# A fused two-layer kernel: the last attention segment without memory, token factors ahead of the output projection, another PSUM bank for the closing pass, closing rows kept in PSUM

## The chip, the cores and the metric

The kernel runs on one core of a Trainium2 chip. The metric is the device time of one execution in microseconds; smaller is better. Matrix products run on TensorE (PE in the profile, its weight loads PEld), element-wise work on VectorE (DVE), ScalarE (ACT) and GpSimd (POOL), and transfers are issued from the queues of SyncE (SP), GpSimd and others. TensorE writes its results to PSUM, eight banks of 512 float32 values for each of 128 partitions; ScalarE and VectorE read them from there.

## What is computed

Two layers, A (attention with a recurrent memory) and B (a gated MLP that mixes over the sequence), each run twice over x of 2048 rows by 512. A goes through 64 segments of 32 rows, and 8 rows of memory pass from each segment to the next, so the segments form a chain. The core of the reference:

```python
def _A_ref(x, mem0, Wq, Wk, Wv, Wo, seg_len):      # 32 heads of 128, M = 8, seg_len = 32
    mem = mem0
    for s in range(n_seg):                          # 64
        h = concatenate([mem, xs], axis=1)          # 8 + 32 rows
        q, k, v = (einsum('btd,dhe->bhte', h, W) for W in (Wq, Wk, Wv))
        p = softmax(where(mask, q @ k * scale, -1e9))
        o = einsum('bhte,hed->btd', p @ v, Wo)
        mem = o[:, :M, :]
        outs.append(o[:, M:, :])
def _B_ref(x, w_in, w_sp, b_sp, w_out):
    z = gelu(einsum('bsd,df->bsf', x, w_in))
    z1, z2 = z[..., :Fh], layernorm(z[..., Fh:])
    return einsum('bsf,fd->bsd', z1 * (einsum('ts,bsf->btf', w_sp, z2) + b_sp), w_out)
x = x + A(layernorm(x)); x = x + B(layernorm(x))    # twice
```

The memory rows that the last segment would pass on go nowhere: only rows 8 to 39 of its output are returned.

## The kernel before

`kernel` builds one program; the function behind it calls `a_block` and `b_block` twice in turn. This document calls the first `a_block` block 1 and the second block 2. On TensorE, VectorE and ScalarE the order of the instructions is the order of the Python calls; on GpSimd and SyncE it is the scheduler's in `a_block`, and in `b_block` SyncE's order is that of the calls too.

`a_block` runs `segment(s, ...)` for s from 0 to 63. In a segment the projections are spread over the array in four column groups of 32, each matmul 32 columns wide by up to 512. A segment goes through these steps:

- Projections psQ (two tiles side by side), psm, psK and psV (line 721, `mm_chunk`). ScalarE casts them to `rows` (line 929), VectorE turns them into QQ and KA (line 932).
- Scores psS (lines 955 and 959), exponentials S (line 964), masked into E (line 967).
- `sums_ahead` and `sums_memory` (lines 990 and 981) give the softmax denominators of the memory queries, `sums_tokens` (line 999) those of the tokens, in psT. `pv` (lines 1007 and 1010) gives the weighted values psO, in two halves of 16 heads each.
- `memory_out` (lines 1024 to 1026) makes the memory's eight rows for uT: ScalarE takes the logarithm and the exponential of its negative, VectorE multiplies.
- The output projection of uT, which holds 24 token rows of the segment before and the 8 memory rows of this one: `wo_pairs` into px (line 798) and `wo_rest` into a corner of psO (line 805).
- The token factors Rt (lines 1090 and 1093), then `fold` (lines 894 and 896), `build_hA` (the memory for the next segment, lines 903 and 904), `store_o` (line 909), and the tokens' products `tok_out` and `last_out` (lines 1029 and 1032) into the next uT and into oB. oB collects the last 8 rows of each segment.

Into this chain other work is woven: `fill()` advances a generator that issues matmuls (projections of old rows, or `y_part`), `spare0` to `spare3` hold statistics and row sums, `copies`, `turns` and `adds` are lists of postponed closures, and `tail` and `loads` issue transfers.

`y_part(G, q, last)` projects the rows collected in oB for a group of 16 segments, a quarter of the heads at a time, into pwB (line 817). Its closure `out` runs with `adds` at the end of the segment and sums the quarters in yB in SBUF (lines 834 and 840), from where `store_last` writes them to o_d. For the last group (`last=True`, segments 61 to 63) three of the row sets get their heads 0 to 23 in three steps, and in each step a fourth column group takes 8 of the heads 24 to 31 of one set. After the loop the statistics and norms of the rows NB-6 and NB-5 are issued (lines 1237 to 1241; `y_norm` is line 249 on VectorE and the store of line 250), and then the closing pass: all 32 heads of the last uT and of the last row set into pw (line 1247). ScalarE copies pw to o_end (line 1250) and VectorE adds two pairs of 32 rows, reading pw and o_end (line 1253). Buffers named `ln_xn`, which `y_norm` writes, are two.

PSUM pools are opened in this order in `a_block`: one pool with accA (pwB and the old rows' projections) and accB (psm, psV, px, pw), one bank each; one with att (psQ, psS, psT; two banks) and the first psO (two banks); one with the second psO (two banks). `b_block` opens a pool of two banks for pg, then one with two buffers of three banks for pz. Its first instructions on TensorE are the 16 projections pz (line 296), each followed by GELU on ScalarE (line 297) and statistics on VectorE (line 300); after the first four, VectorE sums, norms and stores the last rows of x, which come back transposed as `front` for the last projections.

HALVED holds one base-36 digit per segment, the first string for block 1, the second for block 2: that many groups of four 512-wide matmuls in psK and psV are issued as eight of 256. The result is the same.

Of the kernel before, what the change touches and what calls it, by code (L numbers as in the profile page):

```python
# [14 lines left out]
P = 128  # L15
DM = 512
KT = 4
H = 32
# [12 lines left out]
HALVED = (  # L31
    "0380032975297907480707080708080707081904080708070807070807080708",
    "0529482947394739490607082903080708070807070906080729040807070807",
)
# [628 lines left out]
def a_block(tc, c, rows, front, MV_in, RS_in, MV_out, RS_out, ahead, wo, S, first):  # L663
# [6 lines left out]
    with ExitStack() as ctx:  # L670
# [86 lines left out]
        def run(todo):  # L757
            while todo:
                todo.pop(0)()
# [47 lines left out]

        yB, stores = {}, []

        def store_last(G, lo, hi, eng):  # L810
            eng.dma_start(o_d[512 * G + 4 * lo:512 * G + 4 * hi, :].rearrange("(j r) d -> j r d", r=32)[:, 24:32, :], yB[G][lo:hi, :])

        def wo_last(parts, pwB):

            for k, units in enumerate(parts):
                for t, (src, h) in enumerate(units):
                    nc.tensor.matmul(pwB[32 * t:32 * t + 32, :], lhsT=src[:, h, :], rhs=wo.head(h).rearrange("p (kt g el) -> p g kt el", kt=4, g=4),  # L817
                                     start=(k == 0), stop=(k == 7), tile_position=(0, 32 * t))
                yield

        def y_part(G, q, last=False):

            groups = [oBs[G][:, :, 32 * g:32 * g + 32] for g in range(4)]
            if last:
                parts = [[(groups[g], 8 * q + k) for g in range(3)] + [(groups[q], 24 + k)] for k in range(8)]
            else:
                parts = [[(groups[g], 8 * q + k) for g in range(4)] for k in range(8)]
            pwB = accA.tile([P, DM], F32, name="pwB")
            for k, _ in enumerate(wo_last(parts, pwB)):
                if k in (0, 3):  # L830
                    yield

            def add(lo, n, src):
                nc.vector.tensor_tensor(out=yB[G][lo:lo + n, :], in0=pwB[src:src + n, :], in1=yB[G][lo:lo + n, :], op=ALU.add)

            def out():
                n = 96 if last else P
                if q == 0:
                    yB[G] = wk.tile([P, DM], F32, name="yB", bufs=1)
                    nc.vector.tensor_copy(yB[G][0:n, :], pwB[0:n, :])  # L840
                else:
                    add(0, n, 0)
                if last:
                    if q == 2:
                        store_last(G, 0, 64, nc.sync)
                    add(32 * q, 32, 96)
                    if q == 2:
                        store_last(G, 64, 96, nc.sync)
                elif q == 3 and G < NB // 4 - 2:
                    stores.append(lambda: store_last(G, 0, P, nc.sync))  # L850
                elif q == 3:
                    store_last(G, 0, P, nc.sync)

            adds.append(out)
            yield

# [55 lines left out]
        def segment(s, fill, spare0, spare1, spare2, spare3, tail, loads):  # L912
# [155 lines left out]
            psT = att.tile([P, 2, 512], F32, name="psT")  # L1068
            sums = (psO[1][:, 0, 384:512].rearrange("p (g n) -> p g n", g=2), psO[1][:, :, 320:384])
            if not (first and s == 0):  # L1070
                fill()
            sums_ahead(sums[0])
            if not (first and s == 0):
                fill()
            pv(0)
            memory_out(0, sums[0])
            spare1(E)
            pv(1)
            sums_memory(1, sums[1])
            sums_tokens(psT)  # L1080
            memory_out(1, sums[1])
            run(copies)
# [5 lines left out]
            beside = nc.scalar.copy(cross[0:64, :], px[64:128, 128:256])  # L1088
            Rt = segp.tile([P, 2, 512], F32, name="Rt", tag="Rt", bufs=1)
            nc.scalar.activation(out=Rt[:], in_=psT[:], func=ACT.Ln)  # L1090
            for r in range(2):
                rt = Rt[:, :, 256 * r:256 * r + 256]
                nc.scalar.activation(out=rt, in_=rt, func=ACT.Exp, scale=-1.0)  # L1093
            run(turns)
            spare2()
            t1 = wk.tile([P, P], F32, name="t1", bufs=1)
# [5 lines left out]
            spare3()  # L1102
            tok_out(0)
            last_out(0)
            fill()
            run(copies)
            tok_out(1)
            last_out(1)
            run(adds)
# [132 lines left out]
        ends = (uT[NSEG % 2], oBs[NB // 4 - 1][:, :, 96:128])  # L1242
        pw = accB.tile([P, 512], F32, name="pw")
        for i in range(H // 2):
            for k in range(4):
                h = 2 * i + k % 2
                nc.tensor.matmul(pw[32 * k:32 * k + 32, :], lhsT=ends[k // 2][:, h, :], rhs=wo.head(h).rearrange("p (kt g el) -> p g kt el", kt=4, g=4),  # L1247
                                 start=(i == 0), stop=(i == H // 2 - 1), tile_position=(0, 32 * k))
        o_sb = segp.tile([P, DM], F32, name="o_end", tag="Rt", bufs=1)
# [45 lines left out]
```

## Time and profile before

| | |
|---|---|
| runs | 1621.28, 1623.1, 1629.42 us; median 1623.1 |
| the profiled execution | 1623.31 us, its span 1621.6 |
| TensorE busy | 1570.2 us, 97% of the span |
| weight loads / VectorE / ScalarE / GpSimd busy | 1003.5 / 1212.6 / 1062.5 / 294.4 us |
| granted TensorE clock, mean | 0.997 |
| closing pass pw, first start of each block | 691.22 and 1481.52 us |
| first pz behind it | 694.98 and 1485.34 us |

Times inside the span are counted from its start. In a row of the chain of waits stand start, length and the engine with the tile and the line. In a row of a timeline stand start, length from the first to the last of the merged instructions, engine, line, operation, output and inputs, and in brackets the idle time ahead of it with what ended it. In a row of windows stand the stretch, its length, then busy time (and count) of TensorE, its weight loads, VectorE, ScalarE and GpSimd, then the granted clock (1.00 is full), the share of the DMA engines and GB/s. A row of a DMA queue has packets, MB and the share of 16 engines' time.

### The profile page before, as it was taken

What the parts mean: (1) busy time and instruction counts of PE and PEld (TensorE: products, weight loads), DVE (VectorE), ACT (ScalarE), POOL (GpSimd) and SP (SyncE); (2) the same over time, 40 slices, a digit from 0 to 9 for tenths busy, and PEclk for the clock granted to TensorE, in tenths of its full rate; (3) what the DMA queues carried; (4) which work ended last, traced back from release to release, by engine and by line L of the source; (5) the groups of instructions that cost most, each with busy time, mean ns of one, the idle gap of its engine ahead of it and who ended that gap; (6) DMA issues with size and microseconds to landing.
All of it is one profiled execution on the core that took longest, in us unless ns stands there. A gap on an engine that the chain in (4) does not pass through costs nothing.

```text
span 1621.6 us, 94617 instructions
## 1 busy us (share of the span) xinstructions
PE 1570.2 (97%) x42719; PEld 1003.5 (62%) x42742; DVE 1212.6 (75%) x3181; ACT 1062.5 (66%) x2278; POOL 294.4 (18%) x604
## 2 busy tenths in 40 slices
PE   3899999999999999999999999999999999999999
PEld 1466666666666666656656666666666666665565
DVE  3677777778887888884467777777888788878722
ACT  2577777777777777662047777777777777776400
POOL 5111111112211221320011111111121112224000
PEclk9899999999999999999999999999999999999999
DMA  9322222123322334276972222221233223425697
GB/s 339 114 50 44 43 43 43 43 43 76 82 58 45 76 92 81 88 174 148 206 194 48 49 45 48 47 47 47 66 92 81 47 65 96 100 56 171 141 201 160
DMA packets 264764, 149.53 MB, mean 92 GB/s; under 512 B 198680, under 2 KB 240784, under 8 KB 264360
## 3 DMA queue, kind: packets, MB, share of 16 engines
q1 hardware_dynamic: 251128, 99.66, 28.4%
q0 software_dynamic: 13232, 43.82, 8.6%
q8 instruction: 335, 5.49, 1.4%
q14 instruction: 69, 0.57, 0.1%
HBM read 59.68 MB, written 37.19 MB: 60 GB/s over the span
## 4 chain that ended last, share of the span: by engine, by line
PE 55%; DVE 1%; ACT 1%; DMA 0%; issue 0%; DVEq 0%
PE pg L396 9%; PE psQ L721 7%; PE psK L721 7%; PE psb L721 5%; PE pz L296 4%; PE px L798 4%; PE psV L721 3%; PE psm L721 3%; PE psO L805 3%; PE py L439 2%; PE psO L1007 2%; PE pwB L817 1%; PE psT L999 1%; PE psS L955 1%; PE pw L1247 0%; PE psO L990 0%
## 5 line engine op out<-in xcount | busy, mean ns | idle before, releaser
L721 PEld LDWEIGHTS <-hT 128*32 128x32 bf16 x14372 | 377.4, 96 | 276.6 <-DVE hT L904 65.1
L932 DVE STREAM_TRANSPOSE QQ<-rows 128x512 bf16<-128x512 bf16 x256 | 179.5, 701 | 19.5 <-ACT rows L929 11.7
L932 DVE STREAM_TRANSPOSE KA<-rows 128x512 bf16<-128x512 bf16 x256 | 175.9, 687 | 13.5 <-ACT rows L929 12.8
L929 ACT CAST rows<-psQ 128x512 bf16<-128x512 f32 x256 | 142.3, 585 | 19.7 <-PE psQ L721 19.4
L396 PE MATMUL pg<-z,wspT 128*128 128x344 bf16 x1024 | 154.3, 309 | 0.0
L1029 DVE TENSOR_TENSOR uT<-psO,Rt 128x384 bf16<-128x384 f32 x256 | 141.4, 552 | 13.2 <-ACT Rt L1093 7.5
L1093 ACT ACTIVATE Rt<-Rt 128x512 f32<-128x512 f32 x256 | 147.3, 622 | 4.1
L1026 DVE TENSOR_TENSOR uT<-psO,Rm 128x128 bf16<-128x128 f32 x256 | 74.7, 292 | 98.1 <-ACT Rm L1025 51.6
L964 ACT ACTIVATE S<-psS 128x224 bf16<-128x224 f32 x256 | 91.6, 358 | 82.0 <-PE psS L959 82.0
L721 PE MATMUL psQ<-Wq_sb,hT 128*32 128x512 bf16 x2048 | 134.8, 381 | 7.3 <-ACT Rt L1090 5.1
L798 PEld LDWEIGHTS <-uT 128*32 128x32 bf16 x4608 | 111.6, 96 | 46.9 <-DVE uT L1026 32.9
L798 PE MATMUL px<-Wo,uT 128*32 128x256 bf16 x3840 | 135.3, 275 | 0.3 <-DVE uT L1026 0.3
L721 PE MATMUL psQ<-Wk_sb,hT 128*32 128x512 bf16 x2048 | 134.5, 381 | 0.0
L721 PE MATMUL psK<-Wk_sb,hT 128*32 128x256 bf16 (+1 forms) x2976 | 134.4, 313 | 0.0
L721 PE MATMUL psK<-Wv_sb,hT 128*32 128x512 bf16 (+1 forms) x2800 | 134.3, 322 | 0.0
L721 PE MATMUL psm<-Wq_sb,hT 128*32 128x512 bf16 x2048 | 134.0, 380 | 0.0
L721 PE MATMUL psV<-Wv_sb,hT 128*32 128x512 bf16 (+1 forms) x2452 | 133.4, 343 | 0.0
L1090 ACT ACTIVATE Rt<-psT 128x1024 f32<-128x1024 f32 x128 | 131.1, 1025 | 3.1
L396 PEld LDWEIGHTS <-wspT 128*128 128x128 bf16 x1024 | 100.2, 98 | 53.2
L805 PE MATMUL psO<-Wo_high,uT 128*32 128x128 bf16 x7168 | 124.7, 219 | 3.2 <-DMA Wo_high<-in_A_Wo_dram 2.3
L888 POOL COPY KX<-old 128x128 bf16<-128x128 bf16 x128 | 70.3, 553 | 314.9 <-PE psS L959 193.1
L888 POOL COPY KX<-front 128x128 bf16<-128x128 bf16 x126 | 67.7, 547 | 296.4 <-PE psS L959 223.0
(194 smaller groups left out, 2896.3 us busy)
## 6 DMA issues: line engine op xcount, KB each, us to landing
o_d<-o_sb SPq DMA_DIRECT2D x126, 64.0 KB
vb_d<-front SPq DMA_DIRECT2D x30, 256.0 KB
VX<-vb_d SPq DMA_DIRECT2D x120, 64.0 KB
ln_x<-xd SPq DMA_DIRECT2D x26, 256.0 KB
y_o<-o_d POOLq DMA_DIRECT2D x22, 256.0 KB, 3.3
xd<-y_o POOLq DMA_DIRECT2D x22, 256.0 KB, 3.5
Wq_sb<-in_A_Wq_dram POOLq DMA_DIRECT2D x8, 512.0 KB, 10.3
Wk_sb<-in_A_Wk_dram POOLq DMA_DIRECT2D x8, 512.0 KB, 11.5
```

The costliest lines, as they stand in the source:

```text
L396: nc.tensor.matmul(pg[t][:, k, 0:344], lhsT=wsp[t][:, st, :], rhs=z(st, 344 * k, 344 * k + 344), start=(st == 0), stop=(st == NT - 1))
L721: mms.append(nc.tensor.matmul(ps[32 * cg:32 * cg + 32, n * k:n * k + n], lhsT=lhs(kt, cg), rhs=r[:, m * k:m * k + m], start=(kt == 0), sto ...
L798: nc.tensor.matmul(px[at:at + 32, 0:256], lhsT=lhs[:, h, :], rhs=wo_rhs(h, slice(k + 2, None, -2) if h % 2 else slice(k, None, 2)), start= ...
L805: nc.tensor.matmul(pw[32 * cg:32 * cg + 32, :], lhsT=lhs[:, h, :], rhs=wo_rhs(h, cg), start=False, stop=(h == H - 1), tile_position=(0, 32 ...
L888: eng.tensor_copy(KX[:, :, r].rearrange("p g (k i) -> p i g k", i=4), bs["KTB"][:, r].rearrange("p (i g) k -> p i g k", i=4)[:, :, :, 8 * ...
L929: return r, mms, nc.scalar.copy(r[:], ps)
L932: nc.vector.transpose(out=QQ[:, j % 2, :, 0:32] if j < 2 else KA[:, j % 2], in_=r[:])
L964: return nc.scalar.activation(out=S[:, r], in_=psS[:, r, 0:224], func=ACT.Exp, scale=scale)
L1026: nc.vector.tensor_tensor(out=hview(uT_cur[:], r, 24, 32), in0=oview(r, 0, 8), in1=rm.rearrange("p g (n q) -> p g n q", q=8), op=ALU.mult)
L1029: nc.vector.tensor_tensor(out=hview(uT_nxt[:], r, 0, 24), in0=oview(r, 8, 32), in1=rview(r, 0, 24), op=ALU.mult)
L1090: nc.scalar.activation(out=Rt[:], in_=psT[:], func=ACT.Ln)
L1093: nc.scalar.activation(out=rt, in_=rt, func=ACT.Exp, scale=-1.0)
```

## The change

Four things are changed in `a_block`, and the strings.

- The last segment (`ends_here`) leaves out `sums_ahead`, `sums_memory` and both `memory_out`. The eight rows of uT that they filled keep older values; the output rows made from them are overwritten by `store_last`, as before.
- In the last segment the token factors are taken right behind psT, half 1 ahead of half 0, and the products `tok_out` and `last_out` of both halves go ahead of `fold` on VectorE.
- The closing pass writes to the first half of a tile of att instead of accB, and begins with heads 16 to 31.
- For the last group the three quarters keep one tile pwB. Its first three row sets accumulate in PSUM over all three segments; the fourth column group, started anew in each, is copied to yB by ScalarE. Only in segment 63 VectorE adds the 96 rows once, and one store of 96 rows follows.
- HALVED has new digits.

```diff
@@ -29,8 +29,8 @@
 WO_PAIR = 18
 LATE_STATS = 14
 HALVED = (
-    "0380032975297907480707080708080707081904080708070807070807080708",
-    "0529482947394739490607082903080708070807070906080729040807070807",
+    "5392919491949293909080707080708070807080708070708070807070807190",
+    "8084929392939050070807080708070708070807080707080708070807080708",
 )
 OLD_SIZES = (H * P, 8 * DH, H * 32, H * 32)
 ORDERED = {mybir.EngineType.PE, mybir.EngineType.DVE, mybir.EngineType.Activation}
@@ -805,17 +805,17 @@
                     nc.tensor.matmul(pw[32 * cg:32 * cg + 32, :], lhsT=lhs[:, h, :], rhs=wo_rhs(h, cg),
                                      start=False, stop=(h == H - 1), tile_position=(0, 32 * cg), skip_group_check=True)
 
-        yB, stores = {}, []
+        yB, stores, held = {}, [], {}
 
         def store_last(G, lo, hi, eng):
             eng.dma_start(o_d[512 * G + 4 * lo:512 * G + 4 * hi, :].rearrange("(j r) d -> j r d", r=32)[:, 24:32, :], yB[G][lo:hi, :])
 
-        def wo_last(parts, pwB):
+        def wo_last(parts, pwB, more=False):
 
             for k, units in enumerate(parts):
                 for t, (src, h) in enumerate(units):
                     nc.tensor.matmul(pwB[32 * t:32 * t + 32, :], lhsT=src[:, h, :], rhs=wo.head(h).rearrange("p (kt g el) -> p g kt el", kt=4, g=4),
-                                     start=(k == 0), stop=(k == 7), tile_position=(0, 32 * t))
+                                     start=(k == 0 and not (more and t < 3)), stop=(k == 7), tile_position=(0, 32 * t), skip_group_check=True)
                 yield
 
         def y_part(G, q, last=False):
@@ -825,8 +825,10 @@
                 parts = [[(groups[g], 8 * q + k) for g in range(3)] + [(groups[q], 24 + k)] for k in range(8)]
             else:
                 parts = [[(groups[g], 8 * q + k) for g in range(4)] for k in range(8)]
-            pwB = accA.tile([P, DM], F32, name="pwB")
-            for k, _ in enumerate(wo_last(parts, pwB)):
+            if not last or q == 0:
+                held["pwB"] = accA.tile([P, DM], F32, name="pwB")
+            pwB = held["pwB"]
+            for k, _ in enumerate(wo_last(parts, pwB, last and q > 0)):
                 if k in (0, 3):
                     yield
 
@@ -834,19 +836,19 @@
                 nc.vector.tensor_tensor(out=yB[G][lo:lo + n, :], in0=pwB[src:src + n, :], in1=yB[G][lo:lo + n, :], op=ALU.add)
 
             def out():
-                n = 96 if last else P
                 if q == 0:
                     yB[G] = wk.tile([P, DM], F32, name="yB", bufs=1)
-                    nc.vector.tensor_copy(yB[G][0:n, :], pwB[0:n, :])
+                if last:
+                    nc.scalar.copy(yB[G][32 * q:32 * q + 32, :], pwB[96:128, :])
+                    if q == 2:
+                        add(0, 96, 0)
+                        store_last(G, 0, 96, nc.sync)
+                    return
+                if q == 0:
+                    nc.vector.tensor_copy(yB[G][:], pwB[:])
                 else:
-                    add(0, n, 0)
-                if last:
-                    if q == 2:
-                        store_last(G, 0, 64, nc.sync)
-                    add(32 * q, 32, 96)
-                    if q == 2:
-                        store_last(G, 64, 96, nc.sync)
-                elif q == 3 and G < NB // 4 - 2:
+                    add(0, P, 0)
+                if q == 3 and G < NB // 4 - 2:
                     stores.append(lambda: store_last(G, 0, P, nc.sync))
                 elif q == 3:
                     store_last(G, 0, P, nc.sync)
@@ -1067,18 +1069,34 @@
             Rm = segp.tile([P, 2, 2, 64], F32, name="Rm", bufs=1)
             psT = att.tile([P, 2, 512], F32, name="psT")
             sums = (psO[1][:, 0, 384:512].rearrange("p (g n) -> p g n", g=2), psO[1][:, :, 320:384])
+            ends_here = s + 1 == NSEG
+            Rt = segp.tile([P, 2, 512], F32, name="Rt", tag="Rt", bufs=1)
+
+            def token_factors(rs):
+                nc.scalar.activation(out=Rt[:], in_=psT[:], func=ACT.Ln)
+                for r in rs:
+                    rt = Rt[:, :, 256 * r:256 * r + 256]
+                    nc.scalar.activation(out=rt, in_=rt, func=ACT.Exp, scale=-1.0)
+
             if not (first and s == 0):
                 fill()
-            sums_ahead(sums[0])
+            if not ends_here:
+                sums_ahead(sums[0])
             if not (first and s == 0):
                 fill()
             pv(0)
-            memory_out(0, sums[0])
+            if not ends_here:
+                memory_out(0, sums[0])
             spare1(E)
             pv(1)
-            sums_memory(1, sums[1])
+            if not ends_here:
+                sums_memory(1, sums[1])
             sums_tokens(psT)
-            memory_out(1, sums[1])
+            if ends_here:
+                spare2()
+                token_factors((1, 0))
+            else:
+                memory_out(1, sums[1])
             run(copies)
             px = accB.tile([P, 512], F32, name="px")
             wo_pairs(px, uT_cur)
@@ -1086,13 +1104,15 @@
             wo_rest(pw, uT_cur)
             cross = wk.tile([P, P], F32, name="cross", bufs=1)
             beside = nc.scalar.copy(cross[0:64, :], px[64:128, 128:256])
-            Rt = segp.tile([P, 2, 512], F32, name="Rt", tag="Rt", bufs=1)
-            nc.scalar.activation(out=Rt[:], in_=psT[:], func=ACT.Ln)
-            for r in range(2):
-                rt = Rt[:, :, 256 * r:256 * r + 256]
-                nc.scalar.activation(out=rt, in_=rt, func=ACT.Exp, scale=-1.0)
-            run(turns)
-            spare2()
+            if ends_here:
+                fill()
+                for r in (1, 0):
+                    tok_out(r)
+                    last_out(r)
+            else:
+                token_factors((0, 1))
+                run(turns)
+                spare2()
             t1 = wk.tile([P, P], F32, name="t1", bufs=1)
             fold(px, cross, t1, beside)
             if s + 1 < NSEG:
@@ -1100,12 +1120,14 @@
             if s > 0:
                 store_o(s, pw, t1)
             spare3()
-            tok_out(0)
-            last_out(0)
-            fill()
+            if not ends_here:
+                tok_out(0)
+                last_out(0)
+                fill()
             run(copies)
-            tok_out(1)
-            last_out(1)
+            if not ends_here:
+                tok_out(1)
+                last_out(1)
             run(adds)
             run(turns)
             tail()
@@ -1240,12 +1262,13 @@
         for y in (NB - 6, NB - 5):
             y_norm(y, nc.sync)
         ends = (uT[NSEG % 2], oBs[NB // 4 - 1][:, :, 96:128])
-        pw = accB.tile([P, 512], F32, name="pw")
-        for i in range(H // 2):
+        pw = att.tile([P, 2, 512], F32, name="pw")[:, 0, :]
+        for n in range(H // 2):
+            i = (n + H // 4) % (H // 2)
             for k in range(4):
                 h = 2 * i + k % 2
                 nc.tensor.matmul(pw[32 * k:32 * k + 32, :], lhsT=ends[k // 2][:, h, :], rhs=wo.head(h).rearrange("p (kt g el) -> p g kt el", kt=4, g=4),
-                                 start=(i == 0), stop=(i == H // 2 - 1), tile_position=(0, 32 * k))
+                                 start=(n == 0), stop=(n == H // 2 - 1), tile_position=(0, 32 * k))
         o_sb = segp.tile([P, DM], F32, name="o_end", tag="Rt", bufs=1)
         nc.scalar.copy(o_sb[:], pw[:])
         for k in range(2):
```

## The prediction

> **What bounds the kernel now.** I read the page, then the chain of waits around the end of both attention blocks, then the timelines of TensorE, VectorE and ScalarE there, and last the windows with the granted clock. The page says 97% busy TensorE, so only its idle stretches can be won or added. Most of the change lies in the last three segments and the closing pass of each attention block; the strings HALVED touch all segments. The chain at the end of the second block (start, us, what):
>
> ```profile
> 1460.05 0.60 DVE yB L840
> 1460.67 0.69 DVE yB L834
> ...
> 1461.93 0.67 DVE KA L932
> 1462.60 0.04 issue
> 1462.64 0.28 PE psS L955 x16
> ...
> 1478.28 0.37 issue
> ...
> 1481.04 0.43 DVE uT L1029
> 1481.47 0.04 issue
> 1481.52 3.83 PE pw L1247 x64
> 1485.34 2.43 PE pz L296 x12
> ```
>
> Two things are to be seen: VectorE's closing-row work (yB) delays the key transpose KA, for which the scores wait; and the closing pass pw waits for uT, behind px, ScalarE's Rt and VectorE's statistics. After pw, TensorE goes straight on to pz, the GELU projection of the next block. VectorE in the same stretch:
>
> ```profile
> 1483.68 0.55 DVE L249 TENSOR_SCALAR ln_xn<-rowsB,MV,RS 128x512 bf16<-128x512 f32 x1
> ...
> 1489.02 0.55 DVE L249 TENSOR_SCALAR ln_xn<-y_o,MV,RS 128x512 bf16<-128x512 f32 x1 [3.47 <-DMA xb_d<-ln_xn]
> 1489.60 1.40 DVE L1253 TENSOR_TENSOR o_end<-pw,o_end 32x512 f32<-32x512 f32 x2
> ```
>
> The two additions that read pw out of PSUM (L1253) end at 1491.00, 5.7 us after pz began at 1485.34: they stand behind three row normalisations (L249), the third of which waits until the first one's store has left its buffer. Before, nobody waits for them, since pw has a bank that pz doesn't use. In the first block: L1253 ends at 699.59, pz began at 694.98.
>
> **Part 1, rows kept in PSUM (gain).** Segments 61 and 62 each end with two VectorE instructions on yB (0.68 and 0.69), which fall into the transposes of the next segment. Starts of psQ put segment 61 at 10.02 us and segment 62 at 668.07 to 678.56, 10.49. From psQ to px: 7.39 in segment 61, 7.85 in 62 and 8.42 in 63. The change gives ScalarE one copy of 32x512 instead and VectorE one addition at the very end. Gain 0.46 + 1.03. The copy has no row: 0.26 is the copy of 64x128 (L1088), 0.57 that of 128x512 (L1250); since VectorE takes 0.68 for 32x512 and for 128x512 alike, length decides, and I take 0.55. It goes ahead of the next segment's first cast. In segment 62 ScalarE has 0.28 of idle time before the second and again before the third cast; VectorE, freed of 1.37, then starts its transposes no later than in segment 61, so the copy costs nothing. Without that cover it would cost 0.55.
>
> **Part 2, no memory in segment 63 (gain).** 16 L990 matmuls (0.12) and 4 L981 (0.06) go: 0.18. With part 1, px starts 1.6 earlier: about 685.4 and 1475.4. I count further from px.
>
> **Part 3, factors ahead of Wo.** psT is complete 0.2 after px starts; ScalarE, freed of four Rm steps (about 0.3 each), does Ln 1.02 and then the two Exp, 1.15 together: factors at 1.85 and 2.42. VectorE's two products for half 1 end at 2.5, for half 0 at 3.0. The closing pass now takes heads 16 to 31, half 1, first, so half 0 is needed only 1.9 later. TensorE needs px 1.10, L805 0.78, pwB 0.86 = 2.74 and can begin the closing pass there, where before it began 4.24 and 4.50 after px. pw ends at 2.74 + 3.83 = 6.57.
>
> **Part 4, the new bank (loss).** PSUM pools are opened in order: accA and accB take banks 0 and 1, att 2 and 3, the two psO 4 to 7. The next block opens a pool of two banks (0, 1) and then pz's two buffers of three banks, so the first pz lies in 2 to 4. pw moves from accB to att, bank 2. The first pz matmul overwrites pw and so must wait for every reader: ScalarE's copy and both L1253. Behind that wait on TensorE's queue stand all 16 projections, and for them wait GELU and the statistics on VectorE. When do the readers end? VectorE from 3.0 on: fold 0.8, o_sb 0.25, statistics 1.3, to 5.36; ScalarE then does Ln and Exp (0.56, as in block 2 from MV to RS) and only behind them, in program order, the closing copy 0.55, to 6.5; addition 0.68, to 7.2; first normalisation from 7.18. Before it stood at 6.40 and 6.66 after px, so of the 1.6 of parts 1 and 2 it keeps 0.8 and 1.1. The two stores of yB on SP's queue become one, an issue of 0.6 less ahead of the first normalisation's store; I count nothing for it. The third normalisation begins 3.69 (block 1) or 4.79 (block 2) after the first ended, by the rows 693.93 to 697.62 and 1484.23 to 1489.02; then 0.57 and 1.40. Readers end at 13.4 and 14.5 after px: 698.9 and 1490.0. pz is **later by 3.9 and 4.7**, and TensorE idles 6.9 and 8.0 us.
>
> **The clock after the idle time.** Windows of the start of the program (us, TensorE busy first, granted clock in the column 1.00 or 0.50):
>
> ```profile
> 48.50:51.90 3.40, 0.67 (x26) 0.50 (x26) 0.58 (x2) 1.64 (x3) 0.00 (x0) 1.00 0.93 314
> 51.90:55.35 3.45, 1.95 (x44) 1.18 (x47) 1.29 (x6) 0.80 (x2) 0.00 (x0) 0.50 0.05 17
> 55.35:58.75 3.40, 3.40 (x36) 1.27 (x32) 1.55 (x4) 1.13 (x2) 0.00 (x0) 0.50 0.00 0
> 721.50:724.90 3.40, 1.70 (x15) 1.15 (x13) 2.99 (x16) 3.22 (x4) 0.00 (x0) 1.00 0.79 140
> ```
>
> A stretch with 0.67 of 3.40 busy is followed by half the clock; one with 1.70 isn't. Idle times of 7 us contain a whole empty stretch, so pz restarts at 0.50. It stayed so for 3.4 us (45.1 to 48.5) and for 6.0 of work (52.79 to 58.75); half of that is lost, 1.7 to 3.0. I take **2.3 per block**, and as bounds 0 (no drop) and 3.0. The Trainium skill (TensorE: Matmul & The Clock Gate, Part 1: The HAM clock gate) states that the clock halves after one idle window of about 3.4 us and comes back after one busy window; by it the estimate is 1.7 per block, which would take 1.2 off the sum.
>
> **In block 1 a later wait gives some of it back.**
>
> ```profile
> 724.81 9.55 PE L296 MATMUL pz<-front 128*128 128x256 bf16 x80 [1.70 <-DMA front<-xb_d]
> ```
>
> TensorE waits here for rows that VectorE sums and normalises between the statistics of the first four z. TensorE's own delay would be 3.9 + 2.3 - 1.7 = 4.5. The row chain: the first projection (2.4 us, at half clock 4.7) ends at 703.6, the second at 706.05, its GELU (1.32) and statistics (1.1) at 708.6, and only then VectorE sums the first late row, which it began at 703.80 before; the four sums, the norms and the stores follow at their old distance: 4.8 to 5.0 later. The later ends last: block 1 **+5.0**. Block 2 has no such wait: 4.7 + 2.3 = **+7.0**.
>
> **Part 5, HALVED.** The page gives
>
> ```profile
> q8 instruction: 335, 5.49, 1.4%
> ```
>
> 5.49 MB over 335 packets is 16 KB, and over 85,461 weight loads and matmuls 64 bytes: 256 instructions per packet. Counted in order, the stalls "issue" inside segments (405.14, 425.17, 946.07, 1194.64, 1215.00, 1287.71, 1348.04, 1478.65 and others) stand at places 193 to 196 modulo 256, so at packet ends. Segments take 10.00 to 10.02 without one; over that, segments 16 to 61 lose 1.8 us in block 1 and 2.3 in block 2. A halved group adds 8 instructions at no TensorE time (psQ unhalved and psK often halved are both busy 134 us). Old and new digits both bring two segments to about 1280 instructions, five packets; what moves is where the packets end. Old packets last 4.4, 3.4, 4.8, 3.7 and 3.7 us, and the stalls sit on the 3.4 and the 3.7. New ones, by laying the new counts over the old rows: 4.6, 3.4 to 3.7, 4.4, 4.2 and 3.3. The shortest, from the VA loads to the next psQ, lasts 3.2 to 3.5 some 15 times before, with hardly a stall. I take **-1.5**, with the bounds -4.1 (no stall left) and +4.1 (twice as many). The Trainium skill (Runtime: NRT & Kernel Launch, Instruction fetch mechanics) calls the crossing of such a 16 KiB block mostly hidden; then this term is about 0. Here it costs up to 0.5 us where it isn't.
>
> **Sum.** The profiled execution took 1623.31 (span 1621.6); the median of the runs is 1623.1, the same within 0.02%. 5.0 + 7.0 - 1.5 = +10.5: **1633.8 us**.
>
> **Rivals.**
> 1. *The wait comes, the clock stays or the stores land early.* Without the clock term block 1 is bound by the row chain (+2.4) and block 2 by 4.7; with HALVED -1.5 that is +5.6: 1629. For it: idle times of 1.2 and 1.7 us left the clock alone. Against it: these are four times as long. 0.15.
> 2. *Other side: faster.* pz doesn't wait, because the first projection gets the other buffer or the readers come early. Place: the start of pz; price: all of part 4. Then block 2 gains 1.6 + 1.76 = 3.4; block 1 is held by the row chain, which moves 1.1; with HALVED -6.0: 1617.3. It decides once the readers end before pw's end plus 1 us; they end 7 later. For it speaks nothing in the rows but that pool order is argued from code. 0.10.
> 3. *HALVED goes wrong*: twice the stalls on top of the wait, 1633.8 + 5.6 = 1639.4. For it: the new shortest packet is 0.1 shorter than the old. 0.07.
>
> **Chances and range.** The forecast has 0.68. Its own range: pz start 1 us either way in each block, clock 1.7 to 3.0, HALVED by 2.5: 1629 to 1638.5. To hold 8 in 10 of all cases: 1627.5 to 1640. What can be told from no change is 0.5%, 8.1 us: slower means above 1631.2, faster below 1615. Slower: most of the forecast (0.58), rival 3 and a little of rival 1: 0.67. Faster: the tail of rival 2, 0.04. Same: 0.29.
>
> **What would show it.** TensorE's first pz row in each block with 6 to 8 us of idle time put down to DVE o_end; windows of 3.4 us behind it with the clock 0.50; psQ to px near 7.4 in segments 62 and 63 and 7.2 without memory; pw directly behind pwB; the wait for front about as long as before or longer; segments of 10.0. If pz follows pw at once, part 4 is wrong and the time is near 1617. If pz waits 7 us at full clock, rival 1 holds.

## The result, and the profile after

The changed kernel takes 1637.88 us (median of 6 runs, 1633.12 to 1640.96) where the kernel before takes 1622.19 (median of 6 runs, 1620.11 to 1629.42): the ratio is 1.0087, with a 95% interval of 1.0062 to 1.0113. So it is slower, by some 10 to 18 us. The profiled execution took 1640.96 us, its span 1639.2, 17.6 more than the span before.

The chain of waits of the kernel after, at the end of block 2 (start, us, what), shows the new path from the tokens' products to the next block:

```profile
1487.85 0.19 DVE uT L1031
...
1492.04 0.59 ACT yB L842
...
1493.26 0.53 DVE ln_xn L249
...
1495.13 3.67 DMA xb_d<-ln_xn
1498.80 1.85 issue
1500.65 2.72 PE pz L296 x6
```

Before, the chain ran uT, pw, pz on TensorE alone. Now pw isn't in it: between uT and pz stand the closing-row copy, a row norm and the transfer of that norm, then 1.85 us that the profile gives to nothing, in which VectorE ends the third norm and does the two additions. The same end in block 1, first VectorE's timeline, then TensorE's:

```profile
699.67 0.55 DVE L249 TENSOR_SCALAR ln_xn<-y_o,MV,RS 128x512 bf16<-128x512 f32 x1 [1.86 <-DMA xb_d<-ln_xn]
700.25 1.40 DVE L1276 TENSOR_TENSOR o_end<-pw,o_end 32x512 f32<-32x512 f32 x2
```

```profile
701.75 11.69 PE L296 MATMUL pz<-front 128*128 128x512 bf16 x48 [6.71 <-issue]
...
727.26 4.85 PE L296 MATMUL pz<-front,ln_x 128*128 128x256 bf16 x40
731.95 3.27 PE L296 MATMUL pz<-front 128*128 128x256 bf16 x27
```

The additions end at 701.65 and pz begins at 701.75: pz waits for them, though the row names only "issue": the trace has a wait instruction of TensorE at line 296 that ends at 701.70, 0.05 us behind the additions, and in block 2 it is the same (1500.59 behind 1500.55). The 48 matmuls behind the wait take 11.69 us instead of 9.47 for 47. The later wait for front, 1.70 us before, is gone, since TensorE itself is late. Windows there (length, busy TensorE, its weight loads, VectorE, ScalarE, GpSimd, then the granted clock) show why pz is slow:

```profile
695.40:698.80 3.40, 0.00 (x0) 0.00 (x0) 2.38 (x6) 1.28 (x4) 1.76 (x3) 1.00 0.53 157
698.80:702.20 3.40, 0.45 (x2) 0.20 (x3) 1.92 (x3) 1.08 (x1) 2.34 (x5) 0.60 0.48 144
702.20:705.60 3.40, 3.40 (x10) 1.26 (x9) 0.00 (x0) 0.00 (x0) 0.32 (x1) 0.50 0.67 252
```

Behind the counts stand the granted clock, the DMA share and GB/s. After one empty stretch the clock is half, and it stays so until about 4.4 us after pz has begun (0.50 up to 706.0, 1.00 from 706.5).

Cut at the first psQ of segments, the 17.6 us of span lie here. Each entry is the difference of such starts between the two traces.

| stretch | before | after | difference |
|---|---|---|---|
| up to the first psQ | 34.29 | 33.72 | -0.6 |
| block 1, segments 0 to 61 | 633.78 | 637.42 | +3.6 |
| block 1, segment 62 to the first psQ of block 2 | 167.98 | 172.02 | +4.0 |
| block 2, segments 0 to 61 | 621.99 | 625.55 | +3.6 |
| block 2, segment 62 to the end | 163.57 | 170.52 | +7.0 |

Two things had to be explained: the ends (+11.0) and the segments in between (+7.2), whose own instructions differ only in the digits HALVED (and, at the end of segment 61, in the copy of yB).

### The profile page after: what moved, and what is told of

Read it like the earlier page. It is cut to its first block, busy times and chain, and to the rows that moved or that the text cites. A ratio compares the mean times of both kernels' runs of the same rounds, so it can differ in the third digit from the quotient of the medians.

```text
span 1639.2 us, 94617 instructions
## 1 busy us (share of the span) xinstructions
PE 1575.4 (96%) x42742; PEld 1015.3 (62%) x42742; DVE 1208.3 (74%) x3167; ACT 1064.9 (65%) x2276; POOL 290.0 (18%) x604
## 4 chain that ended last, share of the span: by engine, by line
PE 93%; DMA 3%; DVE 2%; ACT 1%; issue 1%; POOL 0%; DVEq 0%; POOLq 0%
PE psQ L721 14%; PE psK L721 13%; PE psb L721 9%; PE pg L396 9%; PE px L798 8%; PE psm L721 7%; PE psV L721 6%; PE psO L805 6%; PE pz L296 5%; PE psO L1009 3%; PE pwB L817 3%; PE py L439 2%; PE psT L1001 2%; PE psS L957 2%; DMA Wk_sb<-in_A_Wk_dram 1%; DMA Wo_high<-in_A_Wo_dram 1%
## 5 line engine op out<-in xcount | busy, mean ns | idle before, releaser
L721 PEld LDWEIGHTS <-hT 128*32 128x32 bf16 x14404 | 386.4, 96 | 272.6 <-DVE hT L906 62.4
L721 PE MATMUL psK<-Wv_sb,hT 128*32 128x256 bf16 (+1 forms) x2812 | 135.0, 321 | 0.0
L805 PE MATMUL psO<-Wo_high,uT 128*32 128x128 bf16 x7168 | 123.5, 219 | 2.4 <-DMA Wo_high<-in_A_Wo_dram 2.4
## 6 DMA issues: line engine op xcount, KB each, us to landing
Wq_sb<-in_A_Wq_dram POOLq DMA_DIRECT2D x8, 512.0 KB, 10.7
```

What stands on the lines that cost most here:

```text
L721: mms.append(nc.tensor.matmul(ps[32 * cg:32 * cg + 32, n * k:n * k + n], lhsT=lhs(kt, cg), rhs=r[:, m * k:m * k + m], start=(kt == 0), sto ...
L805: nc.tensor.matmul(pw[32 * cg:32 * cg + 32, :], lhsT=lhs[:, h, :], rhs=wo_rhs(h, cg), start=False, stop=(h == H - 1), tile_position=(0, 32 ...
```

## The experiments

**e1, the old digits in the changed kernel; e2, the new digits in the kernel before.** At this point the theory (A) was that the digits cost by themselves what the table shows.

```diff
 HALVED = (
-    "5392919491949293909080707080708070807080708070708070807070807190",
-    "8084929392939050070807080708070708070807080707080708070807080708",
+    "0380032975297907480707080708080707081904080708070807070807080708",
+    "0529482947394739490607082903080708070807070906080729040807070807",
```

> The changed kernel with the strings HALVED of before; all else as changed. Theory A (the loss of 15.7 us is the two block ends, +4.1 and +7.3 in the profile, and the new digits, +3.5 and +3.2): block 1 from the first psQ to that of segment 63 takes about 644.2 us again instead of 647.8; block 2 is less sure, since 40 TensorE instructions less in block 1 shift where its packets end; the time falls by 3 to 7 us to about 1632. Theory B (the digits are neutral and the longer segments were the scatter of one execution): 1637 to 1639 and no difference in the segments beyond 1 us. The prediction's own term (new digits better by 1.5): 1639.4.

> The kernel before with the new strings HALVED and nothing else. Theory A: segments of block 1 cost about 3.5 us more, of block 2 about 3; time about 1622 + 3 to 7 = 1625 to 1629. Theory B: within 1 us of the kernel before. The prediction's own term: 1.5 us faster, 1620.7.

e1: 1639.74 us, ratio to before 1.010 (1.0085 to 1.0116): not faster than the change as made. e2: 1632.94, ratio 1.0061 (1.0042 to 1.0079), 10 us slower than before from digits alone. Neither is what theory A or its rival said. e1's time is near the 1639.4 that the prediction's own term gave for it: the old digits come out 1.9 us slower than the new ones in the changed kernel, though the two intervals overlap. By place, e1 has a good block 1 (segments 2 to 61 in 602.9 us against 605.0) and a bad block 2 (segments 0 to 61 in 626.5, against 625.5); e2 has a very bad block 2, 634.7, with the same digits that took 625.5 in the changed kernel. What differs between these two for block 2 is only what stands ahead of it: the changed kernel issues 20 matmuls less in segment 63, which is 40 TensorE instructions with their weight loads, so its block 2 begins 40 places earlier in the packets of 256. This is theory C: a string of digits is worth something only together with the places where the packets end.

**e3, the closing pass back in accB; e4, the closing copy and additions ahead of the last statistics and norms.** Both keep the new digits. In e4 these eight lines move behind the loop:

```diff
# e3
-        pw = att.tile([P, 2, 512], F32, name="pw")[:, 0, :]
+        pw = accB.tile([P, 512], F32, name="pw")
# e4
-        for k in range(3):
-            y_stats(NB - 5, k)
-        run(copies)
-        for y in (NB - 6, NB - 5):
-            y_norm(y, nc.sync)
         ends = (uT[NSEG % 2], oBs[NB // 4 - 1][:, :, 96:128])
...
+        for k in range(3):
+            y_stats(NB - 5, k)
+        run(copies)
+        for y in (NB - 6, NB - 5):
+            y_norm(y, nc.sync)
         _act_table(nc, GELU_SET)
```

> The changed kernel with the closing pass back in accB, new digits kept. Theory A: pw now waits for fold, the last reader of px, which ended 1.3 us after pw began in block 1 and in block 2; pz follows pw at once, with no idle time and no half clock behind it: pz 5.3 to 5.6 us earlier, another 2.3 us from the clock, of which block 1 gives up to 1.7 back at the later wait for front. About -6 and -8: 1624. Rival (the wait of pz isn't pw's bank but the loading of the next stage, an activation table or front rows): pz stays 6 us or more behind pw and the time stays within 2 us of 1637.9.

> The changed kernel, bank and digits kept, with only the order changed: the closing copy and the two additions stand ahead of the last row statistics and of the last two row normalisations. Theory A (pz waits for the additions, which stand behind a normalisation that waits for a store): the additions end about 2.9 us after pw in block 1 instead of 6.7, some 3.5 in block 2 instead of 8.4; gain 3.8 and 4.8, and 2.3 more in each block if the shorter idle time leaves the clock alone: 1625 to 1629. Rival (pz waits for something else, the additions are not last): pz starts where it did, 6.7 and 8.4 us behind pw, time 1637.9. If the additions still end late because the closing copy on ScalarE is late, the gain is under 2 us.

e3: 1622.32 us, ratio 1.0001 (0.9991 to 1.0012). The whole loss is gone by moving one tile. e4: 1628.07, ratio 1.0028 (1.0018 to 1.0037): with the bank of the change, the order on VectorE alone gives back 10 of the 15.7 us. In e4 pz begins 6.97 and 6.36 us after pw instead of 10.38 and 12.00, so it does follow the additions. VectorE and TensorE of e4 in block 2:

```profile
1487.12 1.40 DVE L1271 TENSOR_TENSOR o_end<-pw,o_end 32x512 f32<-32x512 f32 x2
```

```profile
1488.62 1.86 PE L296 MATMUL pz<-front 128*128 128x512 bf16 x4 [2.69 <-issue]
```

The shorter idle times of 3.34 and 2.69 us still cost the clock: windows of 2 us show 0.50 behind both. In e3 TensorE's timeline has in block 1, and then in block 2:

```profile
693.35 9.75 PE L296 MATMUL pz<-front 128*128 128x512 bf16 x47
```

```profile
1495.56 9.47 PE L296 MATMUL pz<-front 128*128 128x512 bf16 x47 [0.35 <-DMA front<-xb_d]
...
1512.22 9.47 PE L296 MATMUL pz<-front 128*128 128x512 bf16 x47 [2.54 <-DMA front<-xb_d]
```

No idle time ahead of pz, but in block 2 TensorE is now early enough to meet the rows: 2.9 us of waits for front that were hidden before. So e3 is where the gain of the other parts went next.

**e5, the sums of segment 63 issued again without use, on e3; e6, the same with the old digits.** This puts back the 40 instructions and nothing else.

```diff
-            if not ends_here:
-                sums_ahead(sums[0])
+            sums_ahead(sums[0])
...
-            if not ends_here:
-                sums_memory(1, sums[1])
+            sums_memory(1, sums[1])
```

> The kernel of e3 (closing pass in accB, new digits) in which segment 63 still issues the 20 small matmuls of sums_ahead and sums_memory, whose results nothing reads: 40 TensorE instructions, 0.18 us of work in each block, so that block 2 begins 40 instructions later in its packets, as in the kernel before. Theory C (what the digits are worth depends on where the packets of 256 TensorE instructions end, so a shift of 40 instructions spoils digits that fit): block 2 from the first psQ to that of segment 63 takes about 645 us, as in the run with the new digits alone (645.4), instead of 633.1; block 1 stays at 646; time 1634. Rival (the digits cost what they cost by themselves, and the 645 came from elsewhere in the kernel before): block 2 633 to 636, time 1622 to 1625.

> As e5, with the strings HALVED of before as well: digits and places of the packet ends are both those of the kernel before. Theory C: block 1 644 to 646, block 2 632 to 633 as before; time 1619 to 1621. Rival (old digits are worse in the changed kernel, as the run with old digits suggested with 1639.7 against 1637.9): 1624.

e5: 1633.04, ratio 1.0047 (1.0033 to 1.0062). Work of 0.18 us per block made the kernel 7.5 us slower than e3 by the two ratios, each to the kernel before in its own session, and 10.7 by the medians. Block 2's segments 0 to 61 take 632.9 instead of 623.0. TensorE's waits within block 2 (what it waited for: us in total, times, longest) have two lines at the head in e5 that e3 doesn't have at all:

```profile
PE psO L805 <- issue: 3.3, 9, 0.5
PE px L798 <- DVE uT L1028: 2.9, 2, 1.6
```

Counted in order (weight loads, matmuls and semaphore waits of TensorE), the six largest of these L805 stalls stand at places 193 and 194 modulo 256, at packet ends: the shift has brought packet ends into the output projection, where 56 small matmuls pass in 0.78 us. e6: 1624.33, ratio 0.9994 (0.998 to 1.0008); block 2 took 623.2. Theory C holds for block 2 in both. For the time of e6 it gave 1619 to 1621, and the rival 1624: by the median the rival's number came out, and by the ratios e6 is 1 us better than e3, which the intervals can't tell from nothing.

**e7, TensorE kept busy in the wait.** 128 matmuls behind the closing pass, into the half tile that nothing reads.

```diff
+        for n in range(128):
+            m = 512 if n < 96 else 64
+            k = n % 4
+            nc.tensor.matmul(held_pw[32 * k:32 * k + 32, 1, 0:m], lhsT=ends[1][:, n // 4, :], rhs=wo.head(n // 4)[:, 0:m],
+                             start=True, stop=True, tile_position=(0, 32 * k), skip_group_check=True)
```

> The changed kernel with 128 matmuls put behind the closing pass, into the half tile beside pw that nothing reads (96 of 32x512 and 32 of 32x64 columns, 5.5 us of TensorE time and 256 instructions, one whole packet): TensorE works while it would have waited. Theory (the wait of pz stays, but half of the first 4.5 us behind it is lost to the halved clock): pz starts where it did, 6.7 and 8.4 us behind pw, the granted clock stays 1.00, and each block is 2.2 us shorter: 1633.5; up to 1635.5 where block 1 meets the wait for front again. Rival (the clock costs nothing because the next work waits for other engines anyway): 1637 to 1639.

1634.42, ratio 1.0053 (1.0037 to 1.0069). The experiment is impure: the closing copy now waits for the added matmuls too, since they write the same tile, so an idle time of 2.19 us is left ahead of pz in both blocks. In block 2 the clock stays whole, and from the first pz to the next stage's pg take 37.17 us instead of 39.32: the half clock was worth 2.15. In block 1 it falls to half after the same 2.19 us, and the end isn't shorter (162.20 us from psQ of segment 63 to block 2, against 161.62).

**e8, the closing pass in the second psO, and the order of e4.** pw lies in banks 6 and 7, which the first pz (2 to 4) doesn't touch; sums kept, old digits, first norm ahead of the yB addition, third norm in a free buffer.

```diff
-        pw = att.tile([P, 2, 512], F32, name="pw")[:, 0, :]
+        pw = attO[1].tile([P, 2, 512], F32, name="pw")[:, 0, :]
...
-        for y in (NB - 6, NB - 5):
-            y_norm(y, nc.sync)
+        y_norm(NB - 6, nc.sync)
+        rows.y_norm(NB - 5, MV_out[:, NB - 5, 0:1], RS_out[:, NB - 5:NB - 4], nc.sync, rowp.tile([P, 512], BF16, name="rows", tag="rowsQK", bufs=3)[:])
```

> The parts that gain, without those that lose: the closing pass in a tile of the second psO (banks 6 and 7, which tok_out of half 1 frees and only the second pz uses), its copy and additions ahead of the last statistics and norms, the first norm ahead of the yB addition, the third norm in a free rows buffer so that it doesn't wait for a store, old digits and the sums of segment 63 kept so that packets end where they did. Expected by theory: px 1.2 us earlier after psQ, pw directly behind pwB, the first pz directly behind pw, the second pz at most 0.5 us late, no wait for front: psQ of segment 63 to the first psQ of block 2 about 153.3 instead of 157.5, and to the end of the span about 150.5 instead of 153.1; with segments as before 1614 to 1618. Rival (front rows are bound by something other than the third norm's store): the ends gain 1 to 2 us only, 1619 to 1621.

1627.36, ratio 1.0011 (1.0001 to 1.0021): a miss. VectorE and TensorE in block 1:

```profile
692.78 1.40 DVE L1272 TENSOR_TENSOR o_end<-pw,o_end 32x512 f32<-32x512 f32 x2
```

```profile
694.28 11.14 PE L296 MATMUL pz<-front 128*128 128x512 bf16 x48 [2.20 <-issue]
```

The additions end at 694.18 and pz begins at 694.28 (in block 2 at 1484.66 and 1484.77), although by the order of the pools pw isn't in pz's banks. The bank numbers come from that order, no trace shows them; but no three neighbouring banks hold both the pw of the change (bank 2) and this one (bank 6). So in this program the first instruction of the stage waits for the readers of any tile that lay where the pool of pz is opened, banks 2 to 7, and not for those of its own three banks alone. accB, which lies outside (bank 0 or 1), is free of that wait, as e3 shows. In block 2 a wait of 2.97 us for front stayed: there GpSimd's queue stood 4.22 us for the store of the buffer that I had given the third norm, with the loads of the late rows behind it.

**e9 and e10, the rows earlier.** pw in accB as in e3; fold ahead of the products of half 0, the yB copy and addition right behind these, and the third norm in a free buffer. e9 has the old digits and the sums kept, e10 the new digits without the sums.

```diff
                 fill()
-                for r in (1, 0):
-                    tok_out(r)
-                    last_out(r)
+                tok_out(1)
+                last_out(1)
...
             fold(px, cross, t1, beside)
+            if ends_here:
+                tok_out(0)
+                last_out(0)
+                run(adds)
```

> The kernel of e6 (closing pass in accB, sums of segment 63 kept, old digits) with four moves in segment 63: fold ahead of the products of half 0, so that pw need not wait for them; the yB copy and addition right behind these products instead of behind the statistics; and the third norm in a free rows buffer, so that it doesn't wait for a store. Theory (what the earlier px and pw gain was given back at the wait for front rows, which hang on the third norm through the load that reuses its input buffer): pw 3.4 us after px instead of 4.0 to 4.5; third norm about 10 us after px instead of 14; no wait for front; psQ of segment 63 to the first psQ of block 2 154.4 instead of 155.4, to the end of the span 150.8 instead of 152.8; time 3 us under that of the kernel before, a ratio of 0.998. Rival (front rows are late for another reason, as in e8): wait of 1.5 us or more for front stays in block 2, ratio 0.999 to 1.001.

> The same moves on the kernel of e3 (closing pass in accB, new digits, no sums in segment 63). Theory: as e9 at the ends, with segments as in e3 (block 1 602.9 for segments 2 to 61, block 2 623 to 625 for 0 to 61): some 3 us more than e9 if the old digits with the old packet places are better by 1.5 in each block, as the profiles so far say. Rival (that difference is scatter): the same time as e9 within 1 us.

e9: 1618.01 us, ratio 0.9964 (0.9949 to 0.9978). e10: 1618.99, ratio 0.9964 (0.995 to 0.9977). Both beat the kernel before, by some 6 us, and the change as made by some 20. For e9 that is about twice the gain that theory gave (a ratio of 0.998). By its trace against that of the kernel before, the ends from segment 62 on give 5.1 us, the segments take back 1.7, and 1.9 lie ahead of the first psQ, where nothing was changed. e10 was to be 3 us slower than e9; the medians are 1.0 apart, as the rival (within 1 us) had it. VectorE and TensorE of e9 at the end of block 2:

```profile
1480.81 0.55 DVE L249 TENSOR_SCALAR rows<-y_o,MV,RS 128x512 bf16<-128x512 f32 x1 [0.18 <-ACT RS L121]
1481.42 1.40 DVE L1277 TENSOR_TENSOR o_end<-pw,o_end 32x512 f32<-32x512 f32 x2
```

```profile
1479.62 9.47 PE L296 MATMUL pz<-front 128*128 128x512 bf16 x48
...
1507.74 9.47 PE L296 MATMUL pz<-front 128*128 128x512 bf16 x48
```

The third norm waits 0.18 us for its scale instead of 5.48 for a store, as in e3; the rows are there when pz asks for them, and neither idle time nor a wait for front is left in block 2 (block 1 keeps 0.72). That gain is shown, but e9 makes several moves at once, and which of them carries how much wasn't taken apart.

Taken from the first psQ of the segments in each trace, us:

| kernel | digits | sums in segment 63 | block 1, segments 2 to 61 | block 2, segments 0 to 61 | psQ of segment 63 to block 2 | psQ of segment 63 to the end |
|---|---|---|---|---|---|---|
| before | old | yes | 601.45 | 621.99 | 157.49 | 153.08 |
| after | new | no | 605.04 | 625.55 | 161.62 | 160.43 |
| e1 | old | no | 602.93 | 626.52 | 161.61 | 160.98 |
| e2 | new | yes | 603.15 | 634.75 | 156.02 | 152.34 |
| e3 | new | no | 602.95 | 623.04 | 154.24 | 154.83 |
| e4 | new | no | 602.81 | 624.28 | 157.66 | 154.98 |
| e5 | new | yes | 603.13 | 632.90 | 156.03 | 151.90 |
| e6 | old | yes | 602.10 | 623.16 | 155.39 | 152.82 |
| e7 | new | no | 604.35 | 624.79 | 162.20 | 157.52 |
| e8 | old | yes | 601.87 | 623.40 | 157.67 | 157.48 |
| e9 | old | yes | 602.22 | 622.45 | 154.76 | 151.65 |
| e10 | new | no | 604.83 | 625.42 | 153.29 | 150.67 |

## Why the prediction was right, and where it was wrong

The forecast of 1633.8 came from 5.0 + 7.0 - 1.5. The direction and the main reason were right; the measured median is 4 us above the forecast, and the last term, -1.5 for the digits, is the main reason. That the time still lies near the forecast is in part luck: the ends were put 1 us too high and the digits some 5 too low, beyond the 2.5 either way that was allowed for them. Step by step:

**Parts 1 to 3 (gains): right.** psQ to px is 7.18 and 7.21 us in segment 63 (predicted 7.2); pw begins 2.64 after px, directly behind pwB (predicted 2.74). Segment 62 is the exception: it gained 0.40 of the predicted 0.46 in block 2 and only 0.09 in block 1, where among others a wait of 0.2 us inside pv came in. Counted from psQ of segment 63, pw starts 2.8 us (block 1) and 3.1 us (block 2) earlier.

**Part 4, the new bank (loss): right in size, too narrow in reason.** Counted from the end of segment 61, pz came 3.7 and 4.7 us later (predicted 3.9 and 4.7), behind idle times of 6.71 and 8.36 (predicted 6.9 and 8.0). e3 and e4 show the cause from two sides: another bank removes it, another order on VectorE most of it. The text argued that pz waits because pw lies in bank 2; e8 shows that it would have waited without an overlap of the two tiles, from a bank elsewhere under the pool.

**The clock: right.** 2.15 us in block 2 by e7, and 2.05 in block 1 by the pz rows (39.57 to pg against 39.22 before, of which 1.70 had been a wait); predicted 2.3. The estimate by the Trainium skill (TensorE: Matmul & The Clock Gate, Part 1: The HAM clock gate) was 1.7, from its one busy window; here the clock stays half for about 4.4 us of work behind these long idle times, and the trace decides.

**Block 1, the later wait: off by 1.** The row chain was to be 4.8 to 5.0 us later and so to bind. It didn't bind: the wait of 1.70 vanished altogether, and block 1's end cost 4.0 instead of 5.0. The sum with TensorE's own delay, 3.7 + 2.05 - 1.7 = 4.05, is the measured one. VectorE's first sum of a late row did start 4.5 later, counted from the end of segment 61 (703.80 before, 711.33 after). But what follows didn't keep its old distance: the load that brings the rows back was issued only 2.3 later (720.47 and 725.88), so the chain moved by less than TensorE's 5.75.

**Part 5, HALVED: the step that failed.** The text took -1.5, from laying the new counts over the old rows and from the claim that the new shortest packet, 3.2 to 3.5 us, lasted long enough. In the profiled pair the segments cost 3.6 and 3.6 more. One execution overstates that. In block 1, whose packets begin at the same place in all kernels, the mean of the table's column is 603.75 for the new digits (seven executions) and 602.1 for the old (five). In block 2 the new digits without the sums give 624.6 (five), the old digits with the sums 622.75 (four). So it is +1.6 and +1.9, and 4.0 + 7.0 + 3.5 = 14.5 us stands beside 15.7 between the medians. The timed pair e9 and e10 puts the whole kernels 1.0 apart only, and their intervals don't exclude none; but in their traces e10's ends from segment 62 on are 1.7 shorter, so that about 2.7 would be left for its segments. So the term has the wrong sign against the kernel before, and its size stays open, at about 1 to 3.5.

Two things in the step were wrong. The first is the claim on the shortest packet. Counted in the traces over segments 2 to 61 (some 149 packets per block, cut at place 193), 10 to 14 packets last under 3.4 us with the old digits at their own count, and 28 to 33 with the new digits in the changed kernel; 22 to 25 of these last under 3.3 us, where the old ones have 6 to 9. In block 2 the time rises with that number: 622 to 623.4 us with 10 to 14 short packets, 623 to 625.6 with 28 to 31, 626.5 with 40 (e1), 632.9 and 634.75 with 54 and 52 (e5, e2). Of the waits themselves the profile names only a part: those put down to "issue" within the segments grew from 0.4 to 1.9 us. The second is that the change itself takes 40 instructions out ahead of block 2, which the text didn't weigh. In the one execution of e1 the old digits cost 626.5 in block 2 at the changed count, instead of 622.75 at their own; the new digits win back part of that, and at the old count they cost 632.9 and 634.75. So within the changed kernel the new digits may even be worth the 1.5 (with the old ones e1 took 1.9 us more, within the intervals); what the prediction set them against was the kernel before. The Trainium skill (Runtime: NRT & Kernel Launch, Instruction fetch mechanics) says that the crossing of a 16 KiB block is mostly hidden; here the same work with packet ends in other places differs by 10 us in 630.

**The rivals.** Rival 3 put HALVED at +4.1 on top of the wait and 1639.4 in all. That is nearer than the forecast: +7.2 in the profiled pair, +3.5 by the means, and 1637.9. Its reason, shorter packets with more stalls, is what the traces show too. The prediction gave it 0.07. Rival 1 (full clock) is refuted by the windows and e7. Rival 2 is the state that e3 makes by hand: pz at once behind pw; its 1617.3 was not reached there, since HALVED didn't give -1.5 and block 2 met the wait for front, but e9 shows 1618.0.

## What to carry to other kernels

Before a result is moved to another PSUM bank, list its readers up to the last one and what stands ahead of them on their engine, and look at what the next stage opens over that bank: in this program all banks below its pool counted. An instruction removed from one stage moves every later packet end of that engine's program; strings tuned to the places of packet ends have to be measured again with each such removal, in several executions. And when TensorE is made earlier, look for the row or transfer that was just hidden: here it took three more small moves before the gain of this change could be seen in the time.

## What the runs showed that was not expected

The halved clock doesn't follow from the length of an idle time alone. In e7 both ends have 2.19 us of idle time ahead of pz. The windows (length, busy TensorE, granted clock, DMA share, GB/s) in block 1, then in block 2:

```profile
702.00:704.00 2.00, 2.00 (x7) 0.64 0.93 227
704.00:706.00 2.00, 2.00 (x7) 0.51 0.57 223
```

```profile
1498.00:1500.00 2.00, 1.68 (x8) 1.00 1.03 330
1500.00:1502.00 2.00, 2.00 (x12) 1.00 0.91 325
```

In e8 it was 2.20 us with half clock in block 1 and 2.42 without in block 2; 2.69 and 3.34 (e4) and 6.71 and 8.36 (after) all brought it on. Of the waits for front, 2.97 (e8, block 2) did and 2.54 (e3, block 2) didn't. The idle time of 1.2 before didn't either. In e8 the first 48 matmuls of pz took 11.14 us at half clock in block 1 and 9.45 in block 2. The Trainium skill (TensorE: Matmul & The Clock Gate, Part 1: The HAM clock gate) speaks of a free-running window of about 3.4 us, and of half clock after one idle window. Idle times shorter than that, which do and don't halve the clock, would agree with it if a window need not be wholly empty; no run here shows where the windows begin.
